# Seven late output tiles get x*Dskip*G from VectorE instead of TensorE, with a new list of the late steps

## The chip, the cores and the metric

One core of a Trainium2 chip runs the kernel. The metric is the device time of one execution in microseconds (us), here the median of several executions. The engines are named as in the profile: PE (TensorE, matmuls; PEld its weight loads), DVE (VectorE), ACT (ScalarE), POOL (GpSimd) and SP (SyncE, which only issues DMAs here).

## The reference

Two sequence mixers run over 2048 rows of 512 features and are mixed row by row with a gate. Cut to what matters:

```python
g = sigmoid((x * gate_w).sum(-1))                 # one number a row
# a: diagonal state-space recurrence over the rows
h_t = Lam_bar * h_{t-1} + B_bar x_t               # complex, 512 states
a_t = 2 * Re(C h_t) + x_t * Dskip
# b: linear attention, 32 heads of 16, with softmax features
phi(u) = concat(softmax(u @ w_phi), softmax(-(u @ w_phi)))
o = (phi(q) kv) / (phi(q) . z + 1e-6)             # kv, z: sums over all rows
b = o @ wo
out = g * a + (1 - g) * b
```

The term of this study is x * Dskip, which in the output is multiplied by g.

## The kernel before

The 2048 rows are cut into 16 tiles of 128 rows. Tile `ti` holds the rows of one residue r = ti // 2 modulo 8 and one half a = ti % 2 of the sequence, so that the recurrence can run over blocks of 8 rows. The tiles are put out in the sequence `order` (line 268); the number n in a step's name counts in it.

A step is a Python generator (`st_y`, `st_o` and so on) that issues a few instructions between two `yield`s. The string `ORDER` (lines 24 to 52) is a hand-written list of tokens, each of which runs one step by one `yield` (lines 817 to 827). `@k` gives the PSUM banks that a step writes, `:D` puts a copy or a scaling on DVE in place of ACT, `:A` puts an output on ACT's queue in place of SP's. PE, DVE, ACT and SP run their instructions in the sequence of this list; POOL is not held to it. An instruction that waits holds up all that is behind it on its engine. There are eight PSUM banks, and a bank can be written again only when what reads it is done.

The steps around the change, for tile n:

- `q` makes the query features' input by PE (four matmuls of 512 columns) and copies them to `Xq[:, n]` on ACT. `h` steps build the states of the recurrence, `c` steps the scaled C.
- `X1` to `X3` and `N1` to `N3` take four tiles of `Xq` at once: a tree of four maxima (or minima) on DVE and a subtraction into `EE`. `E` takes the exponential (four on ACT), `S` sums in a tree of four on DVE, takes a logarithm (`lg`), a difference (`dl`, DVE), an exponential (`rho`, ACT) and a product (`em`, line 560, called S1's to S3's product here), and then issues four DMA transposes to `phT`, one for each tile, on SP.
- `o` multiplies `phT` with `KVm` (two halves `pn0`, `pn1`, four matmuls of 68 columns each), takes a logarithm (`ld`) of the denominators on ACT, copies the numerators (`nu`), makes `rd` on ACT and the normalised rows `on` on DVE. They are transposed to `oT`, by a DMA for n < 12, by PE (`po`) and a copy for n = 12 to 15.
- `y` sums the recurrence's output in a bank `py`: two halves of four matmuls of 512 columns (line 718), then the Dskip group, four matmuls of 128 columns of the transposed x with diagonal matrices `Dd` (line 723).
- `t` adds `oT` times `Wo` (line 766, four matmuls of 512 columns) to the same `py`, scales by the gate `G` into `ot` (line 778 on ACT or line 780 on DVE) and issues the output. The tile n = 14 (`LAST`) is scaled in two halves, one on ACT and one on DVE (lines 772 and 773).

The attention part is scaled by (1 - g)/g in `rd`, so the one factor `G` at the end serves both parts. `Xq` has 16 rows of 512 bf16 numbers in each partition; after `X3` and `N3` it is not used again.

Of the kernel before, what the change touches and what calls it, by code (L numbers as in the profile page):

```python
# [10 lines left out]
ALU = mybir.AluOpType  # L11
AX = mybir.AxisListType
ACT = mybir.ActivationFunctionType
F32 = mybir.dt.float32
# [6 lines left out]
P = 128  # L21
# [15 lines left out]
R6 g23@3 v12@2 c4 c0 c0 g63@5 nA z2 z2 a3 a3 g03@4 xA g03 z2 z2 z2 z2 xA g23 z2 z2 g33@6 c5 v12 z2 z2 g13@0 g13 g63  # L37
g43@4 h32@3 g13 nA g43 h52@2 h52 g33 h32 h61@5 h61 h12@0 c0 g53@4 h12 g33 g53 s4 v14@3 c2 eA eA h42@2 h42 g73@6 g53 eA
eA g73 g73 q10@5 sA h11@0 h11 O h00@4 g73 sA v13@2 h00 v13 a4 z3 sA v15@6 z3 v15 h20@0 h01@4 h30@2 v14 h20 sA h30 z3
h31@6 z3 z3 sA a4 h01 h31 c6 c6 sA q13@3 q13 z3 a4 a4 Y Y h22@0 G q10 z3 z3 G q6@2 q6 h22 z3 z3 sA sA Y Y c1 c1 q9@4  # L40
q8@6 q5@7 h62@3 h41@5 c3 h41 c1 c3 c3 h13@0 h62 q11@2 h13 q11 q8 q12@1 c6 q12 h21@5 q5 h21 h02@2 c7 q4@6 q4 h53@3 h53
h23@1 h23 h33@0 h33 sA q9 h40@7 h40 sA q7@5 h43@6 h63@3 c7 h43 q7 c7 y4@0 y4 sA h63 sA h03@1 END h02 o0@4 o0 X1 N1
o1@7 o1 q14@6 X1 N1 h03 o0@5 X1 o1@2 o1 o1 o0 o0 q15@3 o2@4 o2 o2@7 o2 N1 q15 X1 N1 X1 N1 E1 E1 y2@1 y1@2 y1 E1 E1 q14
X2 y0@5 y0 o1 y4 X2 N2 X2 o0 o0 o3@4 o3 o3@7 o3 o1 o3 y2 X2 N2 o2 X2 N2 S1 S1 N2 S1 o3 S1 N2 S1 S1 o3 y5@3 o2 o2 S1 S1
S1 y1 E2 E2 E2 E2 y9@6 G N3 y5 y5 y3@4 y2 X3 X3 N3 t1 G t1 N3 S1 N3 S2 y9 y9 S2 S2 S1 S1 S2 y3 y3 t3 y0 t0 t0 t2 t2
y6@7 X3 t2:A o4@2 o4 o4@5 o4 o4 y6 y6 t3 X3 o4 X3 o4 S2 S2 t3 o5@1 o5 o5@2 o5 o5 y13@5 y13 o5 N3 o6@4 S2 o6 o6@1 o6 o6
y12@2 o5 y7@4 y7 y12 o6 o6 t4 y7 S2 S2 t4:D S2 E3 E3 E3 E3 S2 o7@1 o7 t5 t5 S3 o7@0 o7 S3 o7 t6 S3 o7 S2 o7 y8@1 o8@3
t6 o8 o8@0 o8 o8 S3 S3 y12 t0:A y11@7 o8 o8 o9@3 o9:D o9@0 o9:D S3 y8 y8 o9 o9 S3 S3 o9 o10@3 y11 o10 o10@0 y11 o10
o10 S3 y14@3 S3 y14 t7 t7:D t8 y14 t8 y15@0 o11@4 S3 o11 o11@1 t9 o12@4 o11:D o11 S3 o10 o10 o12 o12@1 o12 o12 t9:D
o11 y15 o13@4 o13:D o13@6 t6:A o13 o13 o11 o12 y10@1 o14@4 y15 o14:D o12@6 t9 o12:D t7:A t1 y10 y10 o13 o15@4 o15  # L50
o15@6 t4:A t5 o15 o15 t8 o15 t12 t12 t12:A t10 o14@4 o14 o14 t10:D o13@6 t11 o15@2 o15 t10 o13:D t11 t11:A y13 t13 o14
o14@1 t15 t13 t13 t15 t15 o14:D t14 t14 t14:A
"""
H_VECTOR = tuple((r, j) for r in (1, 2, 4, 5, 6) for j in range(4))
OT_PE = (12, 13, 14, 15)
LAST = 14
SPIN_BANK = 7
TWO_PI_LO = float(np.nextafter(np.float32(2.0 * np.pi), np.float32(0.0)))
INV_2PI = float(1.0 / (2.0 * np.pi))
# [10 lines left out]
def kernel(  # L70
# [18 lines left out]
    nc = tc.nc  # L89
    _, S, D = A_x.shape  # L90
# [6 lines left out]
    NR = 8  # L97
# [282 lines left out]
    def st_M():  # L380
        GS = nc.gpsimd.tensor_scalar
        GC = nc.gpsimd.tensor_copy

        def cross(a, b):
            GT(out=outer, in0=a.unsqueeze(2).to_broadcast([P, 2, 2, PT]), in1=b.unsqueeze(1).to_broadcast([P, 2, 2, PT]), op=ALU.mult)

        def cmul(k, a, b):
            cross(a, b)
            GT(out=dl[:, k, :], in0=outer[:, 0, 0], in1=outer[:, 1, 1], op=ALU.subtract)
            GT(out=dl[:, k + 1, :], in0=outer[:, 0, 1], in1=outer[:, 1, 0], op=ALU.add)  # L390

        lb, m2, m4 = dl[:, 0:2, :], dl[:, 2:4, :], dl[:, 4:6, :]
        GT(out=dl[:, 0, :], in0=cs_, in1=r_, op=ALU.mult)
        GT(out=dl[:, 1, :], in0=sn_, in1=r_, op=ALU.mult)
        cmul(2, lb, lb)
        cmul(4, m2, m2)
        cmul(6, m2, m4)
        GT(out=r2_, in0=r_, in1=r_, op=ALU.mult)
        GT(out=r4_, in0=r2_, in1=r2_, op=ALU.mult)
        GT(out=r8_, in0=r4_, in1=r4_, op=ALU.mult)  # L400
        cross(lb, lam)
        GT(out=tb[:, 0, :], in0=outer[:, 0, 0], in1=outer[:, 1, 1], op=ALU.subtract)
        GT(out=tb[:, 1, :], in0=outer[:, 0, 1], in1=outer[:, 1, 0], op=ALU.add)
# [12 lines left out]
        yield

    def st_D():
        v5_ = dgv.rearrange("p (k t a) f -> p k t a f", k=4, a=2)
        b5_ = dgB[:, 0:8].rearrange("p (k a) j h -> p k a (j h)", a=2)  # L420
        for a in range(2):
            nc.vector.tensor_copy(out=v5_[:, :, :, a, :], in_=b5_[:, :, a, :].unsqueeze(3).to_broadcast([P, 4, NT2, 4]))
        VT(out=idn2[:], in0=ident[:, 0:64], in1=ident[:, 64:P], op=ALU.add)
        VT(out=dg[:].rearrange("p k t (a c f) -> p (k t a) c f", f=4, a=2),
           in0=idn2[:].rearrange("p (c f) -> p c f", f=4).unsqueeze(1).to_broadcast([P, 8 * NT2, 16, 4]),
           in1=dgv.unsqueeze(2).to_broadcast([P, 8 * NT2, 16, 4]), op=ALU.mult)
        yield
# [40 lines left out]
    def st_L():  # L468
        pin_act_set()
        tab_g.__exit__(None, None, None)  # L470
        enter("sw", name="ssm", bufs=2)
        yield
# [205 lines left out]
    def st_G():  # L678
        VS(out=nge[:], in0=live["acc"][1][:, 4 * KVW:4 * KVW + NTI], scalar1=-Z_MAX, scalar2=-1.0, op0=ALU.max, op1=ALU.mult)
        yield  # L680
        aexp(out=G[:], in_=nge[:], func=ACT.Exp)
        yield
        VS(out=G[:], in0=G[:], scalar1=1.0, scalar2=None, op0=ALU.add)
        yield
        nc.vector.reciprocal(out=G[:], in_=G[:])
        yield
# [25 lines left out]
    def st_y(n):  # L712
        ti = order[n]
        r, a = ti // 2, ti % 2
        py = bank([P, D], F32, "py")
        live["py", n] = py
        for t in range(NT2):
            MM(out=py[:], lhsT=hs(r, t, slice(a * P, (a + 1) * P)), rhs=C2B[t], start=(t == 0), stop=False)  # L718
            if t % 4 == 3:
                yield  # L720
        for kt in range(KT):
            xs = xT[:, kt, ti * P:(ti + 1) * P]
            MM(out=py[:, kt * P:(kt + 1) * P], lhsT=xs, rhs=Dd[:, kt, :], start=False, stop=False)  # L723
        yield

    def st_o(n):
# [35 lines left out]
    def st_t(n):  # L762
        ti = order[n]
        py, oT = live["py", n], live["oT", n]
        for g in range(HG):
            MM(out=py[:], lhsT=oT[:, g, :], rhs=Wo[:, g, :], start=False, stop=(g == HG - 1))  # L766
        yield
        ot = pools["op"][1].tile([P, D], BF16, name="ot", bufs=14)
        ot2 = pools["op"][1].tile([P, D], BF16, name="ot", bufs=14) if n == LAST else ot

        def ot_halves():
            nc.scalar.mul(out=ot[:, 0:D // 2], in_=py[:, 0:D // 2], mul=G[:, ti:ti + 1])
            VS(out=ot2[:, D // 2:D], in0=py[:, D // 2:D], scalar1=G[:, ti:ti + 1], scalar2=None, op0=ALU.mult)

        if n == LAST:
            ot_halves()
        elif sel["eng"] == "act":
            nc.scalar.mul(out=ot[:], in_=py[:], mul=G[:, ti:ti + 1])  # L778
        else:
            VS(out=ot[:], in0=py[:], scalar1=G[:, ti:ti + 1], scalar2=None, op0=ALU.mult)  # L780
# [8 lines left out]
    small1, big1 = (lambda: sk), (lambda: fk)  # L789
    small3, big3 = (lambda: pools["sq"][1]), (lambda: pools["eq"][1])  # L790
    st = {"V": st_V(), "V2": st_V2(), "U": st_U(), "P": st_P(), "P2": st_P2(), "P3": st_P3(), "P4": st_P4(), "B": st_B(), "gw": st_gw(),
          "M": st_M(), "D": st_D(), "L": st_L(), "G": st_G(), "Y": st_Y(), "END": st_END(), "NR": st_N(0), "NI": st_N(1), "O": st_O()}
    for n in range(8, NTI):
        st[f"l{n}"] = st_l(n)
    for j in range(4):
# [7 lines left out]
    for k in range(4):  # L803
        st[f"J{k}"] = st_J(k // 2, k % 2)
    for n in range(NTI):
        st.update({f"k{n}": st_k(n), f"v{n}": st_v(n), f"q{n}": st_q(n), f"y{n}": st_y(n), f"o{n}": st_o(n), f"t{n}": st_t(n)})
    for n, (t0_, L_) in enumerate(KG):
        st.update({f"x{n}": feat_max(n, t0_, L_, "k", small1, big1), f"n{n}": feat_min(n, t0_, L_, "k", small1),
                   f"e{n}": feat_exp(n, L_), f"s{n}": feat_sum(n, L_, "k", small1), f"a{n}": st_a(n)})
# [51 lines left out]
```

## Time and profile before

| | us |
|---|---|
| median of three runs | 154.85 (154.6 to 154.98) |
| profiled execution, whole time | 155.2 |
| its span (first to last instruction of the program) | 153.1 |
| PE busy | 147.5 |
| DVE busy | 133.1 |
| ACT busy | 129.3 |
| POOL busy | 15.8 |

In a row of the chain of waits stand start, duration, engine, output and line; in a row of a timeline start, duration, engine, line, operation, output and inputs, shapes and how many were merged, and in brackets the idle time of the engine before it with what ended it. In a row of a group the mean duration in ns stands after the total behind the bar. TensorE's granted clock in this execution was 0.998 of full.

### The profile page before, as it was taken

How to read it: one execution, taken by the hardware profiler on the slowest of the kernel's cores; microseconds unless marked ns; L12 is line 12 of the kernel's file. 1: busy time of each engine (PE TensorE's matmuls, PEld its weight loads, DVE VectorE, ACT ScalarE, POOL GpSimd, SP SyncE). 2: the span in 40 equal slices, each digit the busy share in tenths (PEclk: the TensorE clock that was granted, in tenths of full speed). 3: DMA queues.
4: the chain of work that ended last, by engine and by line, in shares of the span. 5: the costliest groups of instructions: out<-in, count | busy, mean ns of one | idle time of the engine just before them, and what ended most of it. 6: DMA issues, size and time to landing. Idle time of an engine off the chain costs nothing.

```text
span 153.1 us, 3382 instructions
## 1 busy us (share of the span) xinstructions
PE 147.5 (96%) x1254; PEld 95.5 (62%) x1254; DVE 133.1 (87%) x304; ACT 129.3 (84%) x279; POOL 15.8 (10%) x43
## 2 busy tenths in 40 slices
PE   7999979999999999999999999999999999999990
PEld 7844434788878986869867656555555555546550
DVE  3799999999999999999999999999999858716441
ACT  3589998999998999999998999699488998618471
POOL 8239980000000000000000000000000000000000
PEclk9999999999999999999999999999999999999999
DMA  4785996494455699720000007911159959989943
GB/s 122 158 215 77 232 160 143 99 79 104 103 107 100 133 222 178 167 97 4 0 0 4 0 0 167 76 37 33 36 98 144 178 125 187 168 139 186 255 145 104
DMA packets 50992, 17.55 MB, mean 115 GB/s; under 512 B 44192, under 2 KB 50976, under 8 KB 50976
## 3 DMA queue, kind: packets, MB, share of 16 engines
q1 hardware_dynamic: 49120, 15.82, 57.0%
q10 hardware_dynamic: 1696, 1.51, 3.1%
q8 instruction: 10, 0.16, 0.5%
q0 software_dynamic: 160, 0.01, 0.2%
q14 instruction: 6, 0.05, 0.2%
HBM read 2.64 MB, written 2.10 MB: 31 GB/s over the span
## 4 chain that ended last, share of the span: by engine, by line
PE 80%; SPq 9%; DMA 8%; issue 1%; DVE 0%; ACT 0%
PE pgq L602 18%; PE py L718 16%; PE py L766 9%; PE pq L476 9%; SPq L230 7%; DMA xT<-in_A_x_dram 5%; PE pk L476 5%; PE pv L476 5%; PE ph L669 4%; DMA phT<-EEq 3%; PE kvacc L579 3%; PE pn L737 3%; PE pgq L607 2%; PE py L723 2%; PE pgq L609 2%; SPq L285 1%
## 5 line engine op out<-in xcount | busy, mean ns | idle before, releaser
L602 PE MATMUL pgq<-xT,BT 128*128 128x256 bf16 x256 | 31.5, 273 | 0.0
L476 PEld LDWEIGHTS <-xT 128*128 128x128 bf16 x192 | 18.1, 97 | 19.2 <-DMA xT<-in_A_x_dram 1.7
L602 PEld LDWEIGHTS <-BT 128*128 128x128 bf16 x256 | 24.6, 98 | 4.1
L139 ACT ACTIVATE EEk<-EEk 128x1024 bf16<-128x1024 bf16 x20 | 20.5, 1082 | 0.0
L120 ACT CAST uv<-pgq 128x512 bf16<-128x512 f32 x28 | 15.9, 605 | 0.7 <-PE pgq L602 0.5
L766 PE MATMUL py<-Wo,oT 128*128 128x512 bf16 x64 | 15.9, 380 | 0.0
L476 PE MATMUL pv<-Wv,xT 128*128 128x512 bf16 x64 | 15.8, 379 | 0.0
L476 PE MATMUL pq<-Wq,xT 128*128 128x512 bf16 x64 | 15.6, 379 | 0.0
L476 PE MATMUL pk<-Wk,xT 128*128 128x512 bf16 x64 | 14.8, 380 | 0.8 <-DMA xT<-in_A_x_dram 0.8
L139 ACT ACTIVATE EEq<-EEq 128x1024 bf16<-128x1024 bf16 x12 | 11.7, 1043 | 0.2 <-DVE EEq L528 0.2
L139 ACT ACTIVATE ld<-pn 128x16 f32<-128x16 f32 x32 | 6.1, 191 | 6.1 <-PE pn L737 4.7
L778 ACT ACTIVATE ot<-py,G 128x512 bf16<-128x512 f32 x11 | 7.4, 689 | 4.0 <-PE py L766 3.6
L591 ACT ACTIVATE phT<-X,dgB 128x512 bf16<-128x512 bf16 x16 | 10.7, 725 | 0.0
L120 ACT CAST nu<-pn 128x256 bf16<-128x256 f32 x27 | 9.9, 381 | 0.0
L745 DVE TENSOR_TENSOR on<-nu,rd 128x512 bf16<-128x512 bf16 x16 | 6.7, 421 | 3.5 <-ACT rd L139 1.8
L120 ACT CAST Xq<-pk 128x512 bf16<-128x512 f32 x15 | 8.6, 597 | 1.3 <-PE pk L476 1.3
L120 ACT CAST vx<-pv 128x512 bf16<-128x512 f32 x16 | 9.1, 603 | 0.4 <-PE pv L476 0.4
L549 DVE TENSOR_TENSOR EEk<-EEk,rck 128x4096 bf16<-128x4096 bf16 (+1 forms) x5 | 9.3, 1859 | 0.0
L120 ACT CAST Xq<-pq 128x512 bf16<-128x512 f32 x16 | 8.9, 609 | 0.2 <-PE pq L476 0.2
L766 PEld LDWEIGHTS <-oT 128*128 128x128 bf16 x64 | 5.5, 97 | 5.7 <-DMA oT<-on 0.8
L737 PEld LDWEIGHTS <-phT 128*128 128x128 bf16 x128 | 6.3, 97 | 3.5 <-DMA phT<-EEq 0.8
L512 DVE TENSOR_TENSOR smk<-smk 128x512 bf16<-128x512 bf16 (+4 forms) x18 | 8.1, 447 | 0.1
(180 smaller groups left out, 323.9 us busy)
## 6 DMA issues: line engine op xcount, KB each, us to landing
X<-HM SPq DMA_DIRECT2D x8, 256.0 KB, 4.4
out_dram<-ot SPq DMA_DIRECT2D x8, 128.0 KB, 2.2
out_dram<-ot ACTq DMA_DIRECT2D x7, 128.0 KB, 2.7
C2r<-in_B_wqkv_dram ACTq DMA_DIRECT2D x2, 256.0 KB, 3.5
Wv<-in_B_wqkv_dram SPq DMA_DIRECT2D x1, 512.0 KB, 4.1
Bn<-in_A_B_re_dram SPq DMA_DIRECT2D x1, 512.0 KB, 6.4
Bn<-in_A_B_im_dram SPq DMA_DIRECT2D x1, 512.0 KB, 7.2
Wo<-in_B_wo_dram SPq DMA_DIRECT2D x1, 512.0 KB, 4.1
```

The lines of the kernel that those rows point to most:

```text
L120: nc.scalar.copy(out=out_ap, in_=in_ap)
L139: ins = nc.scalar.activation(**kw)
L230: nc.sync.dma_start_transpose(out=xT[:, :, ti * P:(ti + 1) * P], in_=x_res[ti // 2, ti % 2])
L476: MM(out=pt[:], lhsT=xT[:, kt, ti * P:(ti + 1) * P], rhs=W[:, kt, :], start=(kt == 0), stop=(kt == KT - 1))
L512: VT(out=dst, in0=cur[:, :, :, 0:n, :], in1=cur[:, :, :, n:2 * n, :], op=op)
L549: VT(out=E5, in0=E5, in1=rc.to_broadcast([P, L, 2 * NB, Dh, 4]), op=ALU.mult)
L591: nc.scalar.mul(out=t_, in_=x_, mul=c_)
L602: MM(out=pg[:, h, :], lhsT=BT[:, kt, 2 * j + h, :], rhs=xT[:, kt, r * NC:(r + 1) * NC], start=(h == 0 and kt == 0), stop=(r % 2 == 0 and k ...
L718: MM(out=py[:], lhsT=hs(r, t, slice(a * P, (a + 1) * P)), rhs=C2B[t], start=(t == 0), stop=False)
L737: MM(out=pn[:, 4 * m:4 * m + 4, :].rearrange("p h e -> p (h e)"), lhsT=ph[:, 4 * hf + m, :], rhs=KVm[:, 4 * hf + m, :], start=(m == 0), st ...
L766: MM(out=py[:], lhsT=oT[:, g, :], rhs=Wo[:, g, :], start=False, stop=(g == HG - 1))
L778: nc.scalar.mul(out=ot[:], in_=py[:], mul=G[:, ti:ti + 1])
```

## The change

For the tiles n = 8 to 13 and 15 (`SKIP_DVE`) the Dskip group of `y` is left out. In its place a step `Z` makes x * G * Dskip in rows on DVE, in float32, and the scaling of `t` becomes one DVE instruction that multiplies `py` by `G` and adds that row tile. What `Z` reads comes by three loads on POOL's queue (`XL`): seven tiles of x in rows and Dskip for all partitions, into rows 0 to 7 of `Xq`; the results take rows 8 to 15, four places used in turn (`GX_SLOT`). The number of instructions on PE falls by 28 matmuls and as many weight loads. From the middle of line 40 on, the list of the steps is another one: another sequence on every engine, other banks, other engines for some copies and other queues for some outputs. The step list of the last tiles runs t14 ahead of t15. The new `XL` and `Z` are entered in the table of steps.

```diff
--- before.py
+++ after.py
@@ -37,23 +37,25 @@
 R6 g23@3 v12@2 c4 c0 c0 g63@5 nA z2 z2 a3 a3 g03@4 xA g03 z2 z2 z2 z2 xA g23 z2 z2 g33@6 c5 v12 z2 z2 g13@0 g13 g63
 g43@4 h32@3 g13 nA g43 h52@2 h52 g33 h32 h61@5 h61 h12@0 c0 g53@4 h12 g33 g53 s4 v14@3 c2 eA eA h42@2 h42 g73@6 g53 eA
 eA g73 g73 q10@5 sA h11@0 h11 O h00@4 g73 sA v13@2 h00 v13 a4 z3 sA v15@6 z3 v15 h20@0 h01@4 h30@2 v14 h20 sA h30 z3
-h31@6 z3 z3 sA a4 h01 h31 c6 c6 sA q13@3 q13 z3 a4 a4 Y Y h22@0 G q10 z3 z3 G q6@2 q6 h22 z3 z3 sA sA Y Y c1 c1 q9@4
-q8@6 q5@7 h62@3 h41@5 c3 h41 c1 c3 c3 h13@0 h62 q11@2 h13 q11 q8 q12@1 c6 q12 h21@5 q5 h21 h02@2 c7 q4@6 q4 h53@3 h53
-h23@1 h23 h33@0 h33 sA q9 h40@7 h40 sA q7@5 h43@6 h63@3 c7 h43 q7 c7 y4@0 y4 sA h63 sA h03@1 END h02 o0@4 o0 X1 N1
-o1@7 o1 q14@6 X1 N1 h03 o0@5 X1 o1@2 o1 o1 o0 o0 q15@3 o2@4 o2 o2@7 o2 N1 q15 X1 N1 X1 N1 E1 E1 y2@1 y1@2 y1 E1 E1 q14
-X2 y0@5 y0 o1 y4 X2 N2 X2 o0 o0 o3@4 o3 o3@7 o3 o1 o3 y2 X2 N2 o2 X2 N2 S1 S1 N2 S1 o3 S1 N2 S1 S1 o3 y5@3 o2 o2 S1 S1
-S1 y1 E2 E2 E2 E2 y9@6 G N3 y5 y5 y3@4 y2 X3 X3 N3 t1 G t1 N3 S1 N3 S2 y9 y9 S2 S2 S1 S1 S2 y3 y3 t3 y0 t0 t0 t2 t2
-y6@7 X3 t2:A o4@2 o4 o4@5 o4 o4 y6 y6 t3 X3 o4 X3 o4 S2 S2 t3 o5@1 o5 o5@2 o5 o5 y13@5 y13 o5 N3 o6@4 S2 o6 o6@1 o6 o6
-y12@2 o5 y7@4 y7 y12 o6 o6 t4 y7 S2 S2 t4:D S2 E3 E3 E3 E3 S2 o7@1 o7 t5 t5 S3 o7@0 o7 S3 o7 t6 S3 o7 S2 o7 y8@1 o8@3
-t6 o8 o8@0 o8 o8 S3 S3 y12 t0:A y11@7 o8 o8 o9@3 o9:D o9@0 o9:D S3 y8 y8 o9 o9 S3 S3 o9 o10@3 y11 o10 o10@0 y11 o10
-o10 S3 y14@3 S3 y14 t7 t7:D t8 y14 t8 y15@0 o11@4 S3 o11 o11@1 t9 o12@4 o11:D o11 S3 o10 o10 o12 o12@1 o12 o12 t9:D
-o11 y15 o13@4 o13:D o13@6 t6:A o13 o13 o11 o12 y10@1 o14@4 y15 o14:D o12@6 t9 o12:D t7:A t1 y10 y10 o13 o15@4 o15
-o15@6 t4:A t5 o15 o15 t8 o15 t12 t12 t12:A t10 o14@4 o14 o14 t10:D o13@6 t11 o15@2 o15 t10 o13:D t11 t11:A y13 t13 o14
-o14@1 t15 t13 t13 t15 t15 o14:D t14 t14 t14:A
+h31@6 z3 z3 sA a4 h01 h31 c6 c6 sA q13@3 q13 z3 a4 a4 Y Y h22@0 G q10 z3 z3 G q6@2 q6 sA c3 h22 q5@7 h41@3 h40@0 q11@5
+h62@2 z3 z3 h53@6 h40 h02@4 h33@0 sA q11 h62 h41 h53 c1 q5 h33 c3 c3 Y q4@5 h13@7 h21@2 c1 q4 q12@0 h13 c7 c1 c6 sA sA
+q7@3 Y q12 h03@5 h21 c7 h03 q9@6 h43@0 sA c7 q8@1 h63@5 h23@2 h43 h63 y2@7 q7 sA h23 q9 q15@5 END o1@2 X1 X1 q14@6 X1
+o2@0 X1 q8 o1 o1@2 N1 G h02 o2 o0@1 o0 X1 N1 o0@4 o1 y1@3 N1 q15 y1 y3@5 N1 N1 o3@2 o0 o0 o1 o2@4 X2 X2 o0 E1 X2 o1
+y0@1 y2 y7@0 y3 E1 E1 N2 y1 X2 o2 N2 G N2 E1 X2 y14@4 XL y0 S1 o2 o0 o1 S1 XL S1 S1 y0 o2 N2 o3 t1 q14 y10@6 S1 S1 t1
+o3@2 S1 o3 N2 y14 y5@3 y4@2 S1 o2 X3 o3 X3 y2 S1 X3 y4 t0 E2 y3 N3 E2 X3 E2 E2 t0 t2 y7 t2 o4@1 S1 o4 X3 o4@7 o3 y10
+o4 N3 o5@1 o4 o5 o5@7 y14 N3 y5 S1 S2 o6@1 S2 o3 o4 o5:D S1 o5 S2 N3 o6 y5 S2 y7 S2 o4 y4 N3 o6@7 y6@1 S2 o6 S2 y15@7
+o5 E3 o6 y6 o5 t4 S2 o6 E3 E3 Z9 S2 t3 y6 Z8 t3 t4:D E3 S2 y15 S3 o7@5 t5 o7 y8@2 o7@5 t5 o7 o8@3 y8 o8 o8@5 o6 o7 o8
+S3 o8 S3 o9@3 S3 S3 o9 o7 Z10 S2 t6 y12@5 S2 S3 o8 o7 S3 t6 o9@3 o8 S3 y12 o9 o10@1 y9@3 o10:D o10@1 o10 S3 y9 Z11
+o11@1 t7 t8 o9 o11 o9 t7 o12@1 o10 S3 y13@0 o12 o9 t8:D o11@1 o12@2 o11 S3 o11 o10 o10 y13 o12:D o13@1 o13 S3 o13@2
+o12 o11 t9 o11 y11@1 t9:D t2:A o13 o12 o14@2 o13 o13 t1 t4:A y11 t3 o12@3 o14 o14@2 t7:A t0:A o12 t6:A t10 Z12 o13@3
+Z13 o14:D t12 o14 t8 o15@2 o13 t10:D o15 o15@3 o14 o15 t13 o14@2 o15 t5 t11 t12:D t9 o15 o14 t10 t13:D t13 t11:D t12:A
+o15@2 Z15 o15 t14 t14 t11:A t15 t15:D t14:A t15
 """
 H_VECTOR = tuple((r, j) for r in (1, 2, 4, 5, 6) for j in range(4))
 OT_PE = (12, 13, 14, 15)
 LAST = 14
+SKIP_DVE = (8, 9, 10, 11, 12, 13, 15)
+GX_SLOT = (0, 1, 2, 3, 0, 1, 0)
 SPIN_BANK = 7
 TWO_PI_LO = float(np.nextafter(np.float32(2.0 * np.pi), np.float32(0.0)))
 INV_2PI = float(1.0 / (2.0 * np.pi))
@@ -718,9 +720,27 @@
             MM(out=py[:], lhsT=hs(r, t, slice(a * P, (a + 1) * P)), rhs=C2B[t], start=(t == 0), stop=False)
             if t % 4 == 3:
                 yield
+        if n in SKIP_DVE:
+            return
         for kt in range(KT):
             xs = xT[:, kt, ti * P:(ti + 1) * P]
             MM(out=py[:, kt * P:(kt + 1) * P], lhsT=xs, rhs=Dd[:, kt, :], start=False, stop=False)
+        yield
+
+    def st_XL():
+        rows = x2.rearrange("(a c r) d -> c a r d", r=NR, c=P)
+        nc.gpsimd.dma_start(out=Xq[:, 0:3, :], in_=rows[:, 0, 0:5:2])
+        nc.gpsimd.dma_start(out=Xq[:, 3, :], in_=A_Dskip.unsqueeze(0).to_broadcast([P, D]))
+        yield
+        nc.gpsimd.dma_start(out=Xq[:, 4:8, :], in_=rows[:, 1, 0:7:2])
+        yield
+
+    def st_Z(n):
+        ti = order[n]
+        k = GX_SLOT[SKIP_DVE.index(n)]
+        gx = Xq[:, 8 + 2 * k:10 + 2 * k, :].rearrange("p a d -> p (a d)").bitcast(F32)
+        live["gx", n] = gx
+        nc.vector.scalar_tensor_tensor(out=gx, in0=Xq[:, 4 * (ti % 2) + ti // 4, :], scalar=G[:, ti:ti + 1], in1=Xq[:, 3, :], op0=ALU.mult, op1=ALU.mult)
         yield
 
     def st_o(n):
@@ -774,6 +794,8 @@
 
         if n == LAST:
             ot_halves()
+        elif n in SKIP_DVE:
+            nc.vector.scalar_tensor_tensor(out=ot[:], in0=py[:], scalar=G[:, ti:ti + 1], in1=live["gx", n], op0=ALU.mult, op1=ALU.add)
         elif sel["eng"] == "act":
             nc.scalar.mul(out=ot[:], in_=py[:], mul=G[:, ti:ti + 1])
         else:
@@ -789,7 +811,7 @@
     small1, big1 = (lambda: sk), (lambda: fk)
     small3, big3 = (lambda: pools["sq"][1]), (lambda: pools["eq"][1])
     st = {"V": st_V(), "V2": st_V2(), "U": st_U(), "P": st_P(), "P2": st_P2(), "P3": st_P3(), "P4": st_P4(), "B": st_B(), "gw": st_gw(),
-          "M": st_M(), "D": st_D(), "L": st_L(), "G": st_G(), "Y": st_Y(), "END": st_END(), "NR": st_N(0), "NI": st_N(1), "O": st_O()}
+          "M": st_M(), "D": st_D(), "L": st_L(), "G": st_G(), "Y": st_Y(), "END": st_END(), "NR": st_N(0), "NI": st_N(1), "O": st_O(), "XL": st_XL()}
     for n in range(8, NTI):
         st[f"l{n}"] = st_l(n)
     for j in range(4):
@@ -803,7 +825,7 @@
     for k in range(4):
         st[f"J{k}"] = st_J(k // 2, k % 2)
     for n in range(NTI):
-        st.update({f"k{n}": st_k(n), f"v{n}": st_v(n), f"q{n}": st_q(n), f"y{n}": st_y(n), f"o{n}": st_o(n), f"t{n}": st_t(n)})
+        st.update({f"Z{n}": st_Z(n), f"k{n}": st_k(n), f"v{n}": st_v(n), f"q{n}": st_q(n), f"y{n}": st_y(n), f"o{n}": st_o(n), f"t{n}": st_t(n)})
     for n, (t0_, L_) in enumerate(KG):
         st.update({f"x{n}": feat_max(n, t0_, L_, "k", small1, big1), f"n{n}": feat_min(n, t0_, L_, "k", small1),
                    f"e{n}": feat_exp(n, L_), f"s{n}": feat_sum(n, L_, "k", small1), f"a{n}": st_a(n)})
```

## Prediction

> **What bounds the kernel now.** I read the page first, then the chain of waits from 85 us on (up to there both orders are the same), then the rows of DVE, ACT and SP in that stretch. The page:
>
> ```profile
> DMA  4785996494455699720000007911159959989943
> PE 80%; SPq 9%; DMA 8%; issue 1%; DVE 0%; ACT 0%
> ```
>
> The chain of waits in order of time (start, us, what):
>
> ```profile
> 86.91 3.45 PE pq L476 x16
> ...
> 105.63 0.22 PE py L723 x4
> 105.86 0.26 PE pn L737 x8
> ...
> 116.83 4.36 DMA phT<-EEq
> 121.24 0.43 PE pn L737 x8
> ...
> 147.79 1.74 PE py L766 x8
> ...
> 150.06 0.48 DVE ot L773
> ```
>
> The reader is to see that the chain stays on PE. Four matmuls of 512 columns cost 0.86 us (3.45 for 16), a Dskip group of four (L723) 0.22, a group of four pn 0.13. From 86.91 to 149.53 (147.79 + 1.74) lie 62.62 us. The old order holds there 58 groups of four by 512 (10 q, 32 y halves, 16 t: 50.1), 16 Dskip groups and four transposes by PE (20 x 0.22 = 4.4), 32 pn groups (4.1) and twelve h groups (30 matmuls of 256 columns, at half of a 512's 0.216: 3.2), 61.85 in all. So PE waited only 0.77 us; what shortens PE's work shortens the time, as long as no new wait comes in.
>
> **The change, part by part.** The profiled execution took 155.2 us, its span is 153.1; the median of the runs is 154.85. I work out a difference against the span and put it on the median.
>
> *Removed:* seven Dskip groups, 7 x 0.22 = 1.54 us of PE. By work alone t15's last matmul, now last, ends at 86.91 + 61.85 - 1.54 = 147.22. I call that time of a PE group its place.
>
> *Added on DVE:* seven Z and seven scalings with an addend (scalar_tensor_tensor), the latter in place of two scalings on DVE (t9, t10) and five on ACT (t8, t11, t12, t13, t15); t7's goes from DVE to ACT. DVE's groups with comparable shapes (mean ns after the bar's first figure):
>
> ```profile
> L780 DVE TENSOR_SCALAR ot<-py,G 128x512 bf16<-128x512 f32 x4 | 3.0, 748 | 4.1 <-PE py L766 4.1
> L449 DVE SCALAR_TENSOR_TENSOR psi<-iot,ssm_par,kk 128x256 f32<-128x256 f32 x4 | 1.9, 474 | 0.0
> L445 DVE TENSOR_SCALAR kk<-iot,ssm_par 128x256 f32<-128x256 f32 x4 | 1.3, 349 | 0.1
> L773 DVE TENSOR_SCALAR ot<-py,G 128x256 bf16<-128x256 f32 x1 | 0.5, 483 | 1.8 <-ACT ot L772 1.8
> ```
>
> The three-operand form costs 0.125 us more than the two-operand one at equal shape (474 against 349), and 256 more columns cost 0.265 (748 - 483). So a Z is 0.74 (between 0.47 and 0.87) and a scaling 0.87 (from 0.75, as now, to 1.40, if its 512 columns ran at half rate: 0.87 + 2 x 0.265). I take 0.74 and 0.87, since the only three-operand row shows no half rate. [...]
>
> *Added loads:* 1 MB of x and Dskip on POOL's queue, on which nothing else stands in this stretch. They can start once X1 and N1 have read their rows, about 104 us, where the DMA slices show 1; the first Z comes near 125. I cost them at nothing. If they slow the first two oT, t1 waits; a wait up to 0.9 us there is swallowed by the one at o4 (below), more counts in full.
>
> *The new list* is the larger part. DVE and ACT first; DVE rows in order of time (a price is from start to start; the next one starts some 0.09 before the end, as 103.44 does against 102.84 + 0.69):
>
> ```profile
> 98.02 0.68 DVE L512 TENSOR_TENSOR mxq<-Xq 128x1024 bf16<-128x1024 bf16 x1
> ...
> 102.84 0.69 DVE L512 TENSOR_TENSOR mxq<-Xq 128x1024 bf16<-128x1024 bf16 x1
> 103.44 0.42 DVE L745 TENSOR_TENSOR on<-nu,rd 128x512 bf16<-128x512 bf16 x1
> ...
> 111.86 1.23 DVE L560 TENSOR_TENSOR EEq<-EEq,rhoq 128x2048 bf16<-128x2048 bf16 x1
> ...
> 113.68 0.69 DVE L512 TENSOR_TENSOR mxq<-Xq 128x1024 bf16<-128x1024 bf16 x1
> 114.40 0.43 DVE L512 TENSOR_TENSOR mxq<-mxq 128x512 bf16<-128x512 bf16 x1
> ...
> 115.67 1.22 DVE L512 TENSOR_TENSOR smq<-EEq 128x2048 bf16<-128x2048 bf16 x1
> 116.92 1.61 DVE L512 TENSOR_TENSOR smq<-smq 128x1024 bf16<-128x1024 bf16 x3
> ```
>
> A tree step followed by one that doesn't read it takes 0.60 (102.84 to 103.44), one read at once 0.72 (113.68 to 114.40): 0.12 lost. The old list runs X1 and N1 turn by turn, ten steps in 4.82 (98.02 to 102.84); the new one runs each tree nearly through. The DVE work ahead of X1 is the same, only reordered, so X1 starts at 98.1 again. Up to S1's product (old 111.86) the new list has nine more direct reads (X1 three, N1 three, X2 one, S1's sums two), +1.0, and the moved on (0.33) and G steps cancel within 0.1: 112.9. From there to S2's difference: the product 1.14 (1.23 less the overlap), X3 and N3 4.82 + 4 x 0.12, S2's sums 2.6 (2.86 when all read directly, 115.67 to 118.53), two on 0.66, one nu 0.4: 10.1, so 123.0.
>
> ACT's rows of that stretch:
>
> ```profile
> 115.52 1.29 ACT L778 ACTIVATE ot<-py,G 128x512 bf16<-128x512 f32 x2
> ...
> 122.70 3.90 ACT L139 ACTIVATE EEq<-EEq 128x1024 bf16<-128x1024 bf16 x4
> 126.50 0.16 ACT L139 ACTIVATE ld<-pn 128x16 f32<-128x16 f32 x1
> 126.57 0.36 ACT L120 CAST nu<-pn 128x256 bf16<-128x256 f32 x1
> ...
> 128.13 0.42 ACT L139 ACTIVATE rd<-ld,nge 128x128 bf16<-128x128 f32 x1
> ```
>
> *First gate.* E2 needs N2's subtraction (just ahead of S1's product, done 112.9), ends 116.9, then t0 and t2 are scaled (0.64 each): 118.2. o4's second pn needs t2's bank (7); its place is 117.24 (ahead of it lie 29 groups of 0.864, twelve h, nine pn, four Dskip: 30.33). PE is 0.9 late. S1's first phT is issued 1 us later than now, near 114.2; landing as the one in the chain did (4.36), it comes at 118.5, nearly the same gate.
>
> *Second gate.* S2's difference (0.3, an estimate under on's 0.42) ends 123.3, rho (0.2, as ln) 123.5; E3 (3.90) with o6's rd (0.3) and t3's scaling (0.6) in between ends at 128.3, where the old E3 ended at 126.6. S3's sums wait for it: 131.2. (Z9 and Z8 lie in that wait of DVE, after S2's product and o6's on, 123.6 + 1.14 + 0.33 + 1.5 + t4's 0.75 = 127.3; without it they would cost 1.5.) Then on 0.33, Z10 0.7 and the difference on DVE, rho, t6's scaling and o9's second ln and nu on ACT: 1.3 + 0.25 + 0.64 + 0.4, so 133.7. That empties bank 3 for y9, whose place is 131.97 (15 groups, eleven pn and four transposes by PE from there to 147.22: 15.25): 1.7 late.
>
> *Third gate.* From y9 to o11's second pn lie five groups of 0.864 and four pn, 4.84: 138.5. ACT then does ln, nu, rd of o11 and ln of o12 (0.9), DVE o12's nu (0.4), which empties bank 2 for o13's second pn: 139.85. Behind that lie nine groups of 0.864, five pn, four transposes: 9.3. PE ends at 149.15, with 0.15 for starting again (eight pn took 0.43 behind a wait, else 0.26) 149.3. That is 0.23 earlier than now: the 1.54 saved, less 1.3 of waits.
>
> *The end.* SP's issues of phT (ns min/median/max, first and last start), landings of the oT issued between 130 and 134 us, and of the last outputs (median us):
>
> ```profile
> L564 SPq DMA_TRANSPOSE phT<-EEq x12: 1247/1292/2247, 113.1 to 138.7; - x12
> DMA to landing us min/median/max: 2.7/3.3/4.1
> out_dram<-ot SPq DMA_DIRECT2D x2, 128.0 KB, 1.9
> out_dram<-ot SPq DMA_DIRECT2D x1, 64.0 KB, 1.6
> ```
>
> Now t14's halves follow each other on ACT and DVE, ending at 150.54. In the new list DVE holds, in a row behind o15's on (146.8: o15's pn end 145.3, then ln, nu, rd, on): t13, t11 (0.8 each start to start), Z15 0.7, t14's half 0.4, then t15 (0.87). t15 starts at 149.5 and ends at 150.4, and its output is 128 KB, not 64: 1.9 for 1.6, +0.3. Outputs of early tiles that move behind o11's oT cost nothing while SP and ACT issue them in the last 10 us, under PE's last nine groups; issued behind PE's end, each would add its landing's 1.9.
>
> Sum: last scaling 0.1 earlier, output 0.3 later, 154.85 + 0.2 = 155.05, written **155.0 us**: no change. Bounds: gates away, 153.6; dear scalings, 156.9.
>
> **Rivals.** *PE stays the bound (faster).* The order's gates overlap with work that I put too late, and PE waits no more than now: -1.54, +0.3 at the output: 153.6. For it: the old order, with the same kind of chains, waited only 0.77. Against: three separate gates would have to move by a us or more.
>
> *DVE's last queue (slower).* If a scaling takes 1.40, t13, t11 and t15 grow by 0.53 each and Z15 starts later: +1.6, with t8 and t9 some +0.4 ahead of the third gate: 156.9. It decides from about 0.75 us on, where t15's matmuls and the queue end together. L449 at 0.474 speaks against it, four scalings at 0.748 leave it open. [...]
>
> *A transpose lands late (slower).* o9's oT is issued behind two phT of S3 (1.29 each), whose product ends at 133.9: at 136.6. With 2.7 it lands 139.3, in time; with 4.1 (the largest of those landings) at 140.7, and t9 with the 9.17 us behind it ends PE at 149.9: 155.5.
>
> **How the numbers follow.** No change 0.40, with an own range of 154.5 to 155.4. PE bound 0.22, late transpose 0.25, DVE's last queue 0.13. A measurement of this kernel tells about 0.3% (0.46 us) from no change. Faster: 0.22 and a little of the forecast's low edge, 0.27; slower: 0.32 of the two slow cases (part of the late transpose stays below 0.46); same 0.41. The range leaves out the far half of the PE case and most of the last queue: 153.9 to 156.2.
>
> **What would show it.** Right: PE with 28 matmuls fewer at L723; S1's product near 112.9, E3's end near 128.3, PE waiting ahead of o4's second pn, y9 and o13's second pn, 2 us in all. Wrong: an E3 that ends before 127.3 (then the gain comes through), a scaling at 1.4, POOL loads that land after 120, or PE waiting for oT longest.

## The result and the profile after

| | before | after |
|---|---|---|
| median of four runs, us | 154.72 (154.47 to 154.98) | 159.12 (158.48 to 159.74) |
| ratio, 95% interval | | 1.028 (1.023 to 1.034) |
| profiled execution, whole time | 155.2 | 158.5 |
| its span | 153.1 | 156.7 |

No change was forecast, at 155.0 us; the changed kernel is slower by 4.4 us. The page of after: busy time, PE's slices, and the chain's shares by engine:

```profile
PE 145.6 (93%) x1209; PEld 93.8 (60%) x1226; DVE 139.5 (89%) x311; ACT 129.1 (82%) x279; POOL 17.9 (11%) x46
PE   7899989999999999999999999998997999988690
PE 59%; DMA 13%; DVE 10%; SPq 8%; ACT 4%; issue 1%; ACTq 1%; DVEq 0%
```

PE is busy for 1.9 us less than before (147.5), and its slices show holes in the last quarter. The chain was on PE for 80% and is now for 59%; DMA, DVE and ACT have taken the rest. The chain of waits of after in order of time (start, us, what) names the holes:

```profile
113.03 3.87 ACT EEq L141 x4
116.90 4.63 DMA phT<-EEq
121.58 0.30 PE pn L757 x4
...
133.22 4.00 DMA oT<-on
137.26 1.04 PE py L786 x4
...
140.31 0.43 DVE nu L124
140.78 0.29 PE pn L757 x4
...
142.05 3.42 DMA phT<-EEq
145.50 0.34 ACTq L808
145.88 0.50 ACTq L808
146.42 0.59 ACT oT L122
...
151.84 0.48 ACT ot L792
```

The first three pieces that are off PE are of the kinds that the prediction worked out: S1's phT, an oT of the tiles o8 to o11, a copy of numerators. The fourth is not: a transpose lands, and then two DMA issues on **ACT** follow, and a copy on ACT that PE needs. ACT's rows at that place (in brackets the idle time and what the profile gives for it):

```profile
143.04 0.37 ACT L122 CAST nu<-pn 128x256 bf16<-128x256 f32 x1
145.50 0.88 ACTq L808 DMA_DIRECT2D out_dram<-ot  x2
146.42 0.59 ACT L122 COPY oT<-po 128x512 bf16<-128x512 bf16 x1 [3.01 <-PE py L786]
```

From 143.41 to 145.50 ACT does nothing. Its next instruction in the list is the output of t7, whose tile had been scaled long before. The copy behind it (o12's, which empties the bank for o13's transposes by PE) is put down to PE, but what it copies had been ready since 144.0; the row to look at is the issue in between. The program's own list of instructions shows what the issue waits for (first SP's last transpose of S3, then ACT's output of t7):

```
L566 DMA_TRANSPOSE phT<-EEq 128x8x128 [waits DMAHW5_49,Activation_49]
L808 DMA out_dram<-ot 128x512 [waits DMAHW5_49]
```

In this program the DMAs of SP and ACT take eight semaphores (counters that tell of a landing) in turn, and a DMA that gets one waits until the last DMA on it has landed: of the 88 in the trace that follow another on their semaphore, none is issued ahead of that landing. t7's output got that of S3's last phT, issued at 142.05 and landed 3.42 later, at 145.47. The issue comes 0.03 later.

### The profile page after: what moved, and what is told of

Same layout as the page of the kernel before. It is cut to its first block, busy times and chain, and to the rows that moved or that the text cites. A ratio compares the mean times of both kernels' runs of the same rounds, so it can differ in the third digit from the quotient of the medians.

```text
span 156.7 us, 3328 instructions
## 1 busy us (share of the span) xinstructions
PE 145.6 (93%) x1209; PEld 93.8 (60%) x1226; DVE 139.5 (89%) x311; ACT 129.1 (82%) x279; POOL 17.9 (11%) x46
## 3 DMA queue, kind: packets, MB, share of 16 engines
HBM read 3.69 MB, written 2.10 MB: 37 GB/s over the span
## 4 chain that ended last, share of the span: by engine, by line
PE 59%; DMA 13%; DVE 10%; SPq 8%; ACT 4%; issue 1%; ACTq 1%; DVEq 0%
PE pgq L604 18%; PE pq L478 8%; SPq L232 6%; DMA phT<-EEq 5%; PE py L786 5%; DMA xT<-in_A_x_dram 5%; PE pk L478 5%; PE py L720 4%; PE pv L478 4%; PE ph L671 4%; PE kvacc L581 3%; DMA oT<-on 3%; ACT EEq L141 2%; PE pgq L609 2%; DVE mxq L514 2%; DVE mnq L514 2%
## 5 line engine op out<-in xcount | busy, mean ns | idle before, releaser
L757 PEld LDWEIGHTS <-phT 128*128 128x128 bf16 x128 | 6.9, 97 | 6.2 <-DMA phT<-EEq 1.8
L757 PE MATMUL pn<-KVm,phT 128*128 128x68 bf16 x128 | 7.9, 194 | 1.3 <-DMA phT<-EEq 1.0
```

What stands on the lines that cost most here:

```text
L757: MM(out=pn[:, 4 * m:4 * m + 4, :].rearrange("p h e -> p (h e)"), lhsT=ph[:, 4 * hf + m, :], rhs=KVm[:, 4 * hf + m, :], start=(m == 0), st ...
```

## The experiments

Theory A: the five outputs that the new list puts on ACT (t2, t4, t7, t0, t6) hold ACT, and so o12's copy and PE. Rivals: the late landings of transposes (T), the additions on DVE (D). Later came B (the transposes as a second bound), C (the loads' price) and K (the chain X1 to S3). All times, each ratio to the kernel before on the same chip (the runs were spread over several chips, on which the kernel before took 154.7 to 155.1):

| run | us | ratio to before (95%) |
|---|---|---|
| the change | 159.12 | 1.028 (1.023 to 1.034) |
| outputs on SP | 157.12 | 1.013 (1.008 to 1.018) |
| outputs left out | 158.06 | 1.019 (1.015 to 1.024) |
| one copy ahead | 159.22 | 1.026 (1.019 to 1.034) |
| new list, Dskip on PE | 161.06 | 1.041 (1.037 to 1.045) |
| outputs on SP, X1 and N1 in turn | 156.83 | 1.013 (1.010 to 1.016) |
| outputs on SP, without four oT | 157.05 | 1.014 (1.009 to 1.020) |
| old list, addition on DVE | 156.53 | 1.011 (1.007 to 1.014) |
| same, o13's copy first | 155.59 | 1.005 (1.002 to 1.009) |
| same, without four oT | 154.83 | 0.999 (0.997 to 1.002) |
| same, y6 earlier | 156.07 | 1.008 (1.006 to 1.010) |
| same, loads on SP | 156.66 | 1.011 (1.008 to 1.015) |
| before, without four oT | 155.29 | 1.001 (0.998 to 1.004) |
| before, with the loads | 155.64 | 1.004 (1.001 to 1.006) |
| fitted order | 160.36 | 1.034 (1.029 to 1.039) |

**ACT's outputs on SP**

```diff
-t9:D t2:A ... t4:A ... t7:A t0:A o12 t6:A t10
+t9:D t2 ... t4 ... t7 t0 o12 t6 t10
```

> The changed kernel with the outputs of t2, t4, t7, t0 and t6 issued by SP in place of ACT, at the same places of the list. Theory A (ACT's queue): in the changed kernel's trace ACT stands from 143.41 to 145.50 at the output of t7, and o12's copy behind it starts at 146.42; without these issues the copy starts near 144.3, o13's transposes by PE then wait only for o13's rows (ready at 145.18) and for PE itself (t10's matmuls end at 145.6), and t12 starts near 146.0 in place of 147.49: about -1.4 us, 157.7. Rival T (late transposes through full DMA queues; the wait on ACT only hides them): PE waits for the same transposes, and SP has 13 outputs in place of 8 to issue from 144.8 on, at 0.45 each to 150.7: 159.0 or more.

o12's copy at the same place (S1's product starts 0.50 later here than in the trace of the changed kernel, at 113.41 for 112.91, so all times have to be read 0.5 earlier):

```profile
145.52 0.59 ACT L121 COPY oT<-po 128x512 bf16<-128x512 bf16 x1 [0.64 <-PE po L773]
```

The hole is gone and the copy now waits for PE's transposes alone. The scaling of t14 starts at 150.89 for 151.84, with the shift 1.45 us sooner, and the median falls by 2.0 (the ratio from 1.028 to 1.013). A holds, T in its full form (159.0 or more) falls. But a part of T holds too: PE's wait of 0.58 us for o10's oT is gone. In the changed kernel that oT, issued at 140.72, has two outputs on ACT's queue beside it:

```profile
out_dram<-ot ACTq DMA_DIRECT2D x2, 128.0 KB, 2.7
oT<-on SPq DMA_TRANSPOSE x1, 3.9
```

With the outputs on SP, issued behind the last transposes, it lands in 2.55 us. The run takes both costs away at once. PE still waits 2.1 us for phT in it, 1.1 of them for S3's first, for which the changed kernel did not wait.

**The five outputs left out**

```diff
-t2:A ... t4:A ... t7:A t0:A o12 t6:A
+... o12
```

> The changed kernel without the outputs of t2, t4, t7, t0 and t6 (these five tiles are not written). Theory A: as with SP's issue, -1.4 us, 157.7, with PE's wait for o10's oT (0.58 at 144.71) unchanged. Rival T: the outputs' 128 KB each no longer fill the DMA queues beside the last transposes; o10's oT lands in 2.5 us in place of 3.95 and S3's last phT in 3.2, which takes another 0.6 off: 157.1 or less, and clearly below the run with the outputs on SP.

PE has the same waits as with the outputs on SP, but for S3's first phT, where it waits 1.6 us for 1.1; so it is not the outputs' traffic behind the last transposes that costs. The landing of o10's oT is as T said, and PE's wait of 0.58 for it, which A had unchanged, is gone here too:

```profile
oT<-on SPq DMA_TRANSPOSE x1, 2.5
```

The time is 0.9 above the run with the outputs on SP, where A had the same and T a lower one: 0.5 is the longer wait for S3's phT, 0.3 the close. The program ends 1.59 us after the last output has landed, against 1.27 in the run before. In the trace SP waits at the end for the eight semaphores one by one, 0.06 us each, and here six of these waits came after the last landing.

**One copy ahead of the outputs**

```diff
-t7:A t0:A o12 t6:A t10
+o12 t7:A t0:A t6:A t10
```

> The changed kernel with one copy moved: on ACT, o12's copy runs ahead of the outputs of t7 and t0 instead of behind t7's and t0's; the same DMAs on the same queues. Theory A: the output of t7 still holds ACT until S3's last phT has landed (145.5), but o12's copy is out of its way, o13's transposes start at about 145.7 in place of 147.06: -1.0 to -1.4 us, 157.7 to 158.1, a little dearer than with the outputs on SP, since o14's ld is now behind the wait. Rival T: no change, 159.

A miss: nothing gained.

```profile
145.84 0.58 ACT L121 COPY oT<-po 128x512 bf16<-128x512 bf16 x1 [0.64 <-PE po L773]
146.95 1.37 ACTq L807 DMA_DIRECT2D out_dram<-ot  x3
148.37 0.18 ACT L140 ACTIVATE ld<-pn 128x16 f32<-128x16 f32 x1 [1.94 <-PE py L785]
```

The copy is in time, and the wait has gone to what is next on ACT: o14's `ld`, and behind it DVE's copy of o14's numerators, whose bank PE needs for o15's pn (it waits 1.2 us there, at 149.06). Two more things differ. The semaphores were dealt out anew: t7's output now waits for o11's oT, issued at 144.04 and landed at 146.92, 0.03 ahead of the issue, and no longer for S3's last phT, landed at 146.46. And PE waits 1.57 us for S3's first phT, which landed in 4.83 us (3.39 in the changed kernel). So this run is no clean price of one copy. The mechanism of A stands; the sum in the expectation counted only that copy.

**The new list without the addition on DVE**

```diff
-SKIP_DVE = (8, 9, 10, 11, 12, 13, 15)
+SKIP_DVE = ()
-... XL ... Z9 ... y8 ...
+... y8 y8 ...
```

> The new list with Dskip left on PE for all tiles: no loads, no Z, plain scalings with the same engines. Theory A and the chains of the list: PE has 1.54 us more work, most of which lies in its waits; it comes out at 159.1 to 160.6. Rival D (the additions on DVE are what costs): DVE has 7 x 0.74 us less to do and the time falls to 156 or less.

At 161.06 it is slower still, a little above what was expected and far from D's 156: the additions are not what makes the new list slow. What they cost by themselves this run does not show, since PE has 1.54 us more of work in it and the hold of ACT is longer. The profiled execution had a granted clock of 0.998 and took 159.64 us; the other four had 0.987 to 0.989 and took 161.05 to 161.57. The waits of this run (engine, line, waited for: us in total, times, longest):

```profile
ACT oT L121 <- DMA out_dram<-ot: 3.7, 1, 3.7
PE po L773 <- ACT oT L121: 2.5, 1, 2.5
```

Here the profile names the cause itself: ACT's copy stood behind an output that waited for another output's landing, and PE behind the copy for 2.5 us.

**The old list with the addition on DVE**

```diff
+N1 XL XL E1   S2 S2 Z9 Z8 t4:D   t7 Z10 Z11 t7:D t8 y14 Z12 t8 Z15   o12:D Z13
-o13:D t11 ... t12 t12 t12:A ... o14:D t14
+o13 t11 ... t12 t12 ... t12 ... o14 t15 t15 t14
```

> The old list with only the addition moved to DVE: the seven Dskip groups taken out, the Z steps put into DVE's idle times of the old order (before t4's scaling, before t7's, around t8's, behind o12's copy), the seven scalings on DVE, the copies of o13 and o14 on ACT. Theory A and the chains of the list: the addition itself is nearly free, PE loses 1.54 us of work and waits little more than before: 153.3 to 153.9. Rival D: the additions hold up on and nu on DVE, 155 or more.

A miss of 2.6 us, and on D's side (155 or more). About one of it was this edit's own: ACT copied o15's transposed rows ahead of o13's. That was mended:

> The old list with the addition on DVE, and ACT copies o13's transposed rows ahead of o15's. In the run before this one ACT copied o15's first, and t13 waited 1.17 us for o13's. Expected by all theories: about -1.1 us, 155.4; PE keeps its waits for S1's first phT (0.57) and for o8's oT (0.75).

As expected, 155.59. But it is above the kernel before, with 1.54 us less for PE. PE's waits in it:

```profile
PE py L785 <- DMA oT<-on: 0.8, 1, 0.8
PE pn L756 <- DMA phT<-EEq: 0.6, 1, 0.6
```

Both are for transposes. D has little part in it: DVE's S3 product, behind which the last phT are issued, starts at 132.28 for 132.10 in the kernel before. SP issues the transposes almost without a gap, in this run:

```profile
113.10 6.94 SPq L565 DMA_TRANSPOSE phT<-EEq  x4
...
130.43 5.07 SPq L778 DMA_TRANSPOSE oT<-on  x3
135.60 5.39 SPq L565 DMA_TRANSPOSE phT<-EEq  x4
141.09 2.56 SPq L778 DMA_TRANSPOSE oT<-on  x2
```

That gave theory B: this row, 30 us long (20 transposes, not the 24 of the expectation), is a second bound just under PE's. Three runs leave four of its transposes out.

```diff
+        if n in NO_OT:          # (8, 9, 10, 11)
+            yield
+            return
-        py, oT = live["py", n], live["oT", n]
+        py, oT = live["py", n], live["oT", 7 if n in NO_OT else n]
```

> As the last, without the DMA transposes of o8 to o11 (t8 to t11 multiply o7's oT, so these four tiles of the output are others). Theory B (SP's row of transposes is a second bound, as long as PE's: 24 of them back to back from 113 to 143 us, so that work taken from PE becomes waits for landings): four of 24 fewer is some 5 us of SP, the wait for o8's oT goes, S3's phT come 4 to 5 us earlier, and PE is the bound again with 1.54 less work: 153.4 to 154.0. Rival D (the additions hold DVE, or PE's restarts, cost the gain): within 0.5 of the run with these transposes, 155.

> The kernel before, without the DMA transposes of o8 to o11 (same stand-in). Theory B: here PE is the bound and waits 0.77 us in all; at most that is gained: 154.2 to 155.0. If it falls by 1.5 us or more, the transposes alone were the bound already before, and PE was not.

> The changed kernel with the five outputs on SP, without the DMA transposes of o8 to o11 (same stand-in). Theory B: the waits at S1's phT (1.0) and ahead of it (0.36) stay, since S1's product is still 1 us later than in the old list; the wait for S3's phT (1.1) and the chain behind it go: 157.1 falls to 155.5 to 156.0. Rival D: no change, 157.

B holds for the old list in its direction, not in its size. With the addition on DVE the time falls by 0.8 (to 154.83, not 153.4 to 154.0), PE waits only 0.5 us for phT, and its last matmul ends at 148.74, 0.8 sooner than before's 149.52; of the 1.54 that much arrives. The close takes 0.6 of it back: this program ends 1.52 us after the last landing, the kernel before 0.92. The kernel before does not move: there PE was the bound. On the new list nothing moves either, which was not expected. DVE's S3 product there, and SP's transposes:

```profile
133.16 1.23 DVE L562 TENSOR_TENSOR EEq<-EEq,rhoq 128x2048 bf16<-128x2048 bf16 x1
```

```profile
131.95 1.19 SPq L782 DMA_TRANSPOSE oT<-on  x1
134.45 4.95 SPq L566 DMA_TRANSPOSE phT<-EEq  x3
```

SP stands free until S3's product is done (133.16 + 1.23), and PE then waits 1.4 us for the landing. There the chain X1 to S3 sets the issue, not SP, and the landing took 4.89 us; the other three of S3 took 4.34, 4.14 and 3.14. No run divides the two.

A wait taken away by reordering alone, on the old list:

```diff
-y6@7 X3 t2:A o4@2 o4 o4@5 o4 o4 y6 y6 t3
+y6@7 X3 t2:A y6 o4@2 o4 o4@5 o4 o4 y6 t3
```

> The old list with the addition on DVE (o13's copy ahead of o15's, loads on POOL) and y6's second half ahead of o4's pn, nothing else. Theory B (the row of transposes is a second bound): PE's wait of 0.6 for S1's first phT goes, and the wait for o8's oT, 18 us later, grows by as much, from 0.78 to 1.3; the time stays at 155.4 to 155.7. Rival P (a wait saved is a wait saved): 155.0.

The chain of this run:

```profile
131.82 4.62 DMA oT<-on
136.49 1.04 PE py L785 x4
...
140.70 4.09 DMA oT<-on
144.84 1.04 PE py L785 x4
```

The 0.6 at phT is gone, the wait for o8's oT has grown to 1.1, and a new one of 0.3 has come at o10's. The time is not lower (156.07, above the 155.4 to 155.7 of B and the 155.0 of P). So PE's waits are not separate: they hang on the same row of landings.

**The chain X1 to S3 on the new list**

```diff
-X1 X1 q14@6 X1 o2@0 X1 q8 o1 o1@2 N1 ...
+X1 N1 q14@6 X1 o2@0 N1 q8 o1 o1@2 X1 ...
```

> The changed kernel with the five outputs on SP, and X1 and N1 run turn by turn as in the old list (six direct reads fewer on DVE, 0.12 each). Theory K (the chain X1 to S3 on DVE and ACT sets the landings of phT, and these set PE): S1's product, E2, S1's phT and all behind come 0.7 us earlier, and so does the end: 157.1 to 156.4. Rival F (the landings that count are late for another reason, a fetch of instructions that a transpose meets): the issue moves, the landing that PE waits for does not, 157.0.

S1's product, counted from X1's start, came 0.74 sooner as worked out (14.05 us behind it for 14.79), PE's end 0.4 sooner, and the medians differ by 0.3, within their spread. K and F each hold in part: the landing that PE waits for was again stretched (4.9 us).

**What the loads cost**

```diff
+N1 XL XL E1 E1 y2@1
```

> The kernel before with only the three loads on POOL's queue added, into rows that nothing reads any more (the output is unchanged). In every kernel so far with these loads the program ends 1.27 us or more after the last output has landed, in the ones without them 0.92 to 1.18; POOL's last two semaphore events stand 0.45 apart in the former and 0.08 in the latter. Theory C (the loads cost at the program's close): PE's end unchanged at 149.5, the close 0.37 longer: 155.2 to 155.3 where the kernel before has 154.9. Rival N (the loads are free, as predicted): 154.9. Rival Q (they slow the first transposes and the delay stays): PE's end later by 0.5 or more.

The last output's issue of the kernel before, with the line of its span:

```profile
core 0 of [0], span 153.1 us
...
150.57 0.33 SPq L784 DMA_DIRECT2D out_dram<-ot  x1
```

and with the loads:

```profile
core 0 of [0], span 154.1 us
...
151.14 0.33 SPq L791 DMA_DIRECT2D out_dram<-ot  x1
```

From that issue to the end are 2.92 us (154.06 less 151.14) for 2.57: the close is 0.35 longer, as C says. In the trace, POOL's last two semaphore events stand 0.45 apart for 0.08. The rest of the 0.88 lies ahead of it: PE's last matmul ends at 150.08 for 149.52, later by the 0.5 or more that Q named. Of that, 0.29 is there when X1 starts (98.31 for 98.02), and a wait of 0.4 for an oT is new. Whether the loads bring these about the run does not show. The other way round:

```diff
-        nc.gpsimd.dma_start(out=Xq[:, 0:3, :], in_=rows[:, 0, 0:5:2])
+        for j in range(3):
+            nc.sync.dma_start(out=Xq[:, j, :], in_=rows[:, 0, 2 * j])
```

> The old list with the addition on DVE (o13's copy ahead of o15's), the rows and Dskip loaded by eight smaller loads on SP while it is idle, instead of three on POOL. Theory C: PE's end as before, the close at 0.92 us as in the kernel before, 155.6 falls to 155.2. Rival N: 155.6.

The close is 2.57 again (152.43 to 155.00), so C holds for it; but the time rose by 1.1, since S1's first phT was issued 0.4 later behind its product, and PE's waits for phT and oT grew to 1.0 and 1.1. What was to be gained was lost elsewhere.

**A fitted order**

```diff
-S3 S3 o9 o10@3 y11 o10 o10@0 o10 o10 S3
+S3 S3 o10@3 y11 o10 o10@0 o10 o10 o9:A S3
```

The kernel that this edit changes is the one with the loads on SP. It also puts y6 earlier, o10's last step later and y15's first half ahead of t8.

> As the last, and with PE's and the transposes' order fitted to the shorter PE work: y6's second half ahead of o4's pn (covers the wait of 0.6 for S1's phT), o9's oT issued by ACT where it is idle, so that S3's first phT is issued 1.5 to 2 us sooner, o10's on earlier, y15's first half ahead of t8. Theory B (PE and the row of transposes are bounds of nearly the same length): with both shortened the end comes to PE 149.0 and 154.3 to 154.7 in all, a little under the kernel before. Rival D: 155.2, no gain.

A clear miss, 160.36. SP's transposes, and the one on ACT:

```profile
130.43 2.55 SPq L780 DMA_TRANSPOSE oT<-on  x2
139.43 2.61 SPq L565 DMA_TRANSPOSE phT<-EEq  x2
```

```profile
136.75 1.29 ACTq L780 DMA_TRANSPOSE oT<-on  x1
```

ACT's transpose waited until SP's last one had landed (131.78 + 4.83 = 136.61), and SP's next until ACT's had (139.28). Here the transposes on two queues follow each other with their whole landing in between, and this has a price: S3's first phT was issued at 139.43, for 135.12 with the loads on SP alone. PE waited 2.30 us for it, until 142.67. A second part of the miss is the clock that TensorE was granted (in tenths of full speed, in 40 slices):

```profile
PEclk9999999999999999999999999999999999975899
```

From 141.2 to 148.0 us it stood at 0.50, and four matmuls of 512 columns took 1.90 us for 1.03 later on. By an estimate from these figures that is some 2.6 us of the time. What lowered the clock no run tests; PE had worked for 0.37 us between 140 and 142. The one execution with a granted clock of 1.000 took 158.90. No version that beats the kernel before was found.

## Why the prediction was wrong

**Right: the work and DVE's chain.** The groups of after (a mean in ns behind the total):

```profile
L727 PE MATMUL py<-Dd,xT 128*128 128x128 bf16 x36 | 3.1, 219 | 0.0
L798 DVE SCALAR_TENSOR_TENSOR ot<-py,G,Xq 128x512 bf16<-128x512 f32 x7 | 5.2, 746 | 2.9 <-PE py L786 2.8
L743 DVE SCALAR_TENSOR_TENSOR Xq<-Xq,G 128x512 f32<-128x512 bf16 x7 | 5.0, 744 | 0.0
```

28 matmuls are gone, a Z takes 0.744 (0.74 was said) and a scaling 0.746 (0.87, its lower bound 0.75). The half rate in the 1.40 of DVE's last queue is shown by no run; the seven scalings with an addend took no longer than the plain ones of the kernel before (0.748), so this rival falls. DVE's steps on which the gates were built:

```profile
112.91 1.22 DVE L562 TENSOR_TENSOR EEq<-EEq,rhoq 128x2048 bf16<-128x2048 bf16 x1
...
122.90 0.28 DVE L556 TENSOR_TENSOR dlq<-lgq 128x128 f32<-128x128 f32 x1
...
128.70 1.23 DVE L514 TENSOR_TENSOR smq<-EEq 128x2048 bf16<-128x2048 bf16 x1 [1.49 <-ACT EEq L141]
```

112.9, 123.0 and 128.3 were worked out. The loads slowed the first two oT (3.8 and 3.0 us to landing, 2.4 on the new list without loads), and t1 waited 0.2 for it, ahead of the wait at 121.58 that takes it in, as said.

**Partly right: the gates.** PE's first long wait is 0.96 at 121.58, for S1's third phT, not at o4's second pn for t2's bank. y9 comes at 134.07 for 133.7, but without a wait of its own: PE was late from before. o13's second pn comes at 140.78 for 139.85, and behind DVE's copy of o12's numerators, as said. What was mis-sized is starting again: 0.15 was put in once, but a pn group behind a wait takes 0.29 to 0.30 for 0.13, and a group of 512 columns 1.04 for 0.86 (in the profile, which models the ends of matmuls), and there were seven waits (0.19 to 1.31, 3.9 us together), so some 1.2 us in all.

**The step that failed:** "Outputs of early tiles that move behind o11's oT cost nothing while SP and ACT issue them in the last 10 us, under PE's last nine groups." It priced an output by its issue and its landing, not by what it waits for before it can be issued, not by what stands behind it on ACT, and not by the transposes that land beside it. ACT stood for the output of t7 until 145.50, and PE waited 1.31 us for the copy behind it and 0.58 for o10's oT. With these outputs on SP both waits are gone and the time is 2.0 us lower, 1.45 of it at t14's scaling. It was in sight: DVE's last queue was worked out step by step, ACT's was not.

**The loads "at nothing":** 0.35 us at the close is shown. They did not all start at 104 us: POOL issued the first two at 75.82 and 76.69 and only the third at 104.42. Whether they cost anything on the path of the tiles is open.

**The rivals.** "A transpose lands late" came in part, with o8's oT (4.00, PE 0.19 late) and o10's (0.58) in place of o9's, which landed in 2.57 us but was issued at 138.04, 1.4 later than said. "PE stays the bound" is what the runs speak against most: even on the old list, PE's shorter work runs into a row of landings, and of 1.54 us 0.8 arrive at best, with four transposes left out.

The sum: 4.1 us lie between forecast and result by the medians. By the spans of the profiled executions it is 3.3 (156.67 for 153.14 + 0.2); the profiled one of the changed kernel was the fastest of its four. PE's last matmul ends at 152.67, 3.4 us behind the 149.3 of the prediction. Behind it the last scaling ends 0.3 sooner than said (0.82 us after PE for 1.1), and the close is longer by the loads' 0.35. Of PE's lateness, the seven waits and their starting again make 5.1 us, where 2.1 were forecast. The hold of ACT is 1.5 of these, o10's oT 0.75; the rest is divided by the trace alone, and no run takes it apart.

## What to carry to other kernels

An output moved to a busy engine's queue is priced by the wait ahead of its issue (here 2.09 us of ACT, ahead of t7's output): look up which earlier DMA must have landed, what stands behind it on that engine, and which transposes are under way beside it. Look again after each change of the list, since another list can give it another semaphore, as with one copy moved. Where a bound is shortened, find the next one first; here a row of transposes was so near under PE that work taken from PE, or a wait taken out of its order, came back at the next landing (of 1.54 us 0.8 arrived at best, and y6 moved earlier took 0.6 off one wait for 0.6 more at two others). When the profile puts a wait down to an engine that had long been done, read the DMA issue just ahead.

## What the runs showed of the hardware

**A packet on the instruction queue and a late landing come together.** Two windows of the changed kernel's DMA (queue, packets, MB, share of 16 engines; and issues with KB each and us to landing): the first has one packet on the queue of instructions, the second, of 4 us, has none.

```profile
q8 instruction: 1, 0.02, 4.2%
oT<-on SPq DMA_TRANSPOSE x1, 3.9
phT<-EEq SPq DMA_TRANSPOSE x1, 4.1
```

```profile
q1 hardware_dynamic: 2667, 0.66, 85.0%
phT<-EEq SPq DMA_TRANSPOSE x3, 3.3
oT<-on SPq DMA_TRANSPOSE x1, 2.5
```

4.2% of sixteen engines over 1.6 us is 1.1 us on one engine. Over all sixteen traces of this study, the 55 phT that have a packet of 16 KB on that queue between issue and landing took 4.40 us in the median, the 137 others 3.29; of the oT, 34 took 3.90 and 146 took 2.51. Each kernel has one such packet that starts between 114 and 121 us and one between 132 and 138, so one usually falls on S1's phT and one near S3's. This is a coincidence in time seen often; no run moved the packet by itself.

**Outputs beside a transpose.** An oT with outputs on ACT's queue beside it landed in 3.95 us in the changed kernel and in 3.69 in the new list with Dskip on PE; with the outputs on SP or left out it took 2.55 and 2.47.

**Loads on POOL's queue lengthen the close.** From the last landing to the end are 1.27 to 1.28 us in the eight kernels here that have these loads and leave no DMA out, and 0.91 to 0.92 in the four without them. SP's waits for its eight semaphores, 0.06 each, count when they come after the last landing.
